# Attention and a squared-ReLU FFN on one core: the ffn matmuls read their moving columns in pairs, one from each half of the block

## The chip, the cores and the metric

The kernel runs on one core of a Trainium2 chip. The time is that of one execution on the device in microseconds; the median of several runs is given. TensorE (PE) multiplies: a matmul loads a stationary operand of up to 128 x 128 (the weights; PEld in the profile) and streams the columns of a moving operand past it, and the sums go into a PSUM bank of 512 float32 columns. VectorE (DVE) and ScalarE (ACT) do the elementwise work, read PSUM and write SBUF. SyncE (SP) issues most of the transfers to and from HBM. Each engine works through its own list of instructions in order, and they wait for each other through semaphores.

## The reference

Cut to what is computed:

```python
# q, k, v: (8, 12, 448, 64)
scores = scale * np.matmul(q, k.transpose(0, 1, 3, 2)) - np.log(448)
attn = 1.0 / (1.0 + np.exp(-scores))
attn_out = np.matmul(attn, v)
x = attn_out.transpose(0, 2, 1, 3).reshape(3584, 768)
# w_in: (768, 2048), w_out: (2048, 768), s, b: one number each
h = x @ w_in
r = np.maximum(h, 0.0)
g = s * (r * r) + b
out = g @ w_out          # (3584, 768)
```

## The kernel before

**Attention** (lines 344 to 632) runs over 24 quads of heads (8 batches x 3). For each quad it makes the scores (line 420), the sigmoid on ScalarE (line 400), the product with the values (lines 454 and 463), and stores the result as x in HBM (line 471), one row of the feature dimension per partition, tokens along the free dimension. Beside it VectorE and ScalarE convert the weights and make sums of weight blocks, which go to HBM.

**The ffn** works on blocks of 512 tokens (`TB`), seven in all. Every operand is float32 that is split into a high part, rounded to a type that TensorE reads at full rate (`F32R`), and a low part, the rest. A product of two such numbers is three matmuls: high by high, high by low, low by high (`PARTS`).

Block 0 goes the plain way. `ffn1` (line 556) makes one row block of h from 6 blocks of 128 features x 3 parts, 18 matmuls, for each of 16 row blocks of the hidden layer (line 563). `activate` (line 751) makes g of it. `ffn2` (line 761) adds g into six PSUM banks `pos`, 18 matmuls again (line 765). At the end ScalarE copies the six banks out, in pairs (lines 844 to 847), and the pool of banks is opened anew for the next stage.

Blocks 1 to 6 go in two groups of three (`threes`). For each group the matrix product is made by a scheme with 15 products of sums of blocks in place of 18. The first layer (lines 1080 to 1127) has 15 products in four pieces `p`, 60 units of 12 matmuls (line 1095: 2 halves `j` x 2 feature blocks `c` x 3 parts), in the order `L1`. A unit reads one tile of weight sums, `wu`, which `weights()` (line 864) takes from a ring of seven tiles that are fetched six units ahead (`AHEAD`). Products that share a bank pair follow each other in it (`CHAINS_1`), and `results_1` (line 960) copies or adds the bank into the tiles `G`. The second layer (lines 1210 to 1251) has 60 units of 12 matmuls too (line 1225), in the order `L2`: 15 products, each with its four pieces one after the other. `prep` (line 1016) makes the operand sums and splits them three units ahead (`LEAD`). When a product is done, `results_2` (line 1138) copies or subtracts its bank pair (`bk`, 128 x 2 x 512) into the output tiles `C`, and `out_store` (line 836) sends them to HBM. There are four bank pairs.

The last unit of all (`end`) is cut into three pieces (`LAST`, line 875): feature block 0 with 512 columns, and feature block 1 in two halves of 256. Each piece has a bank pair of its own, is subtracted from `C["t"]` and stored by itself (lines 1231 to 1237), so that the end of the kernel is short.

The moving operand of each ffn matmul is 512 neighbouring float32 words of each partition: `x0[h][xi][:, cc, :]` (line 564), `g[:, gi, :]` (line 766), `opd[i][xi][:, c, :]` (line 1096), `g[gi][:, f, tk]` (line 1226). The column of the PSUM bank is that of the token.

The helpers `add` and `sub` (lines 177 to 181) are where VectorE's additions and subtractions are recorded, so those rows have lines 178 and 181; ScalarE's copies of banks in `results_2` have line 1141, its split casts lines 678 and 680.

Of the kernel before, what the change touches and what calls it, by code (L numbers as in the profile page):

```python
# [36 lines left out]
TB = 512  # L37
# [57 lines left out]
def sigmoid_attention_relu2_ffn(  # L95
# [10 lines left out]
    nc = tc.nc  # L106
# [7 lines left out]
    KC = NCC // 3  # L114
# [59 lines left out]
    def f32(ap):  # L174
        return ap.bitcast(F32)

    def add(o, x, y):
# [378 lines left out]
    def ffn1(f, w):  # L556
        ph = ps_h.tile([P, TB], F32, tag="ph", name=f"ph_{f}")
        m = 0
        for c in range(NCC):
            h, cc = divmod(c, HC)  # L560
            k, kc = divmod(c, KC)
            for wi, xi in PARTS:
                nc.tensor.matmul(  # L563
                    ph, w[:, k, wi, kc * P : (kc + 1) * P], x0[h][xi][:, cc, :],
                    start=m == 0, stop=m == 3 * NCC - 1,
                )
                m += 1
        cx.free(w)
        return ph
# [191 lines left out]
    def ffn2(w, g, first, last):  # L761
        for e in range(NCC) if not last else evict:
            k, kc = divmod(e, KC)
            for i, (wi, gi) in enumerate(PARTS):
                nc.tensor.matmul(  # L765
                    pos[e], w[:, k, wi, kc * P : (kc + 1) * P], g[:, gi, :],
                    start=first and i == 0, stop=last and i == 2,
                )
# [75 lines left out]
    for e in evict[::2]:  # L844
        outs.append(slot(f"o_{e}"))
        nc.scalar.copy(outs[-1][:, 0], pos[e])
        nc.scalar.copy(outs[-1][:, 1], pos[e + 1])
    todo[10].pop(0)()
# [102 lines left out]
    for n, blocks in enumerate(threes):  # L951
# [128 lines left out]
        for u, (i, p) in enumerate(L1):  # L1080
# [10 lines left out]
            for j in range(2):  # L1091
                m = 0
                for c in range(KC):
                    for wi, xi in PARTS:
                        nc.tensor.matmul(  # L1095
                            bk[:, j], wt[:, j, wi, c * P : (c + 1) * P], opd[i][xi][:, c, :],
                            start=i == ch[0] and m == 0,
# [39 lines left out]

        def results_2(i, bk):
            def copy(c):
                C[c] = slot(f"C_{n}_{c}")  # L1140
                nc.scalar.copy(C[c], bk)

# [12 lines left out]
            elif i == 10:  # L1155
                sub(C[5], C[5], bk)
                put(5)
            elif i == 7:
                C[2] = slot(f"C_{n}_2")
                sub(C[2], C["u"], bk)  # L1160
                copy(0)
                put(2)
            elif i == 1:
                sub(C[0], bk, C[0])
                put(0)
# [4 lines left out]
            elif i == 4:  # L1170
                sub(C[8], bk, C[8])
            elif i == 3:
                sub(C[7], C[7], bk)
                put(7, True)
            elif i == 12:
                C[1] = C.pop("u")
                sub(C[1], bk, C[1])
                put(1)
            elif i == 11:
                C[3] = slot(f"C_{n}_3")  # L1180
                sub(C[3], C["t"], bk)
                put(3)
            elif i == 14:
                copy("v")
            elif i == 0:
                sub(C["v"], C["v"], bk)

# [11 lines left out]
            elif n + 1 < len(threes):  # L1199
                C[4] = C.pop("t")  # L1200
                for e in range(KC):
                    sub(C[4][:, e], C[4][:, e], bk[:, e])
                    m, k = divmod(4, 3)
# [6 lines left out]
        for j, (i, p) in enumerate(L2):  # L1210
# [8 lines left out]
            for e, tk in LAST if end else [(e, slice(TB)) for e in range(KC)]:  # L1219
# [3 lines left out]
                for f in range(2):  # L1223
                    for m, (wi, gi) in enumerate(PARTS):
                        nc.tensor.matmul(  # L1225
                            o, wt[:, f, wi, e * P : (e + 1) * P], g[gi][:, f, tk],
                            start=(end or i == ch[0] and p == 0) and f == 0 and m == 0,
# [3 lines left out]
                if end:  # L1231
                    x = C["t"][:, e, tk]
                    sub(x, x, o)
                    t0 = blocks[1] * TB
                    nc.sync.dma_start(
                        out[(KC + e) * P : (KC + e + 1) * P, t0 + tk.start : t0 + tk.stop], x
                    )
            if n + 1 == len(threes) and j + 2 == len(L2):
                sub(C["t"], C["t"], bk)
            for t in g:  # L1240
# [49 lines left out]
```

## Time and profile before

| what | value |
|---|---|
| median of 3 runs | 1039.26 us (1038.59 to 1039.77) |
| span of the profiled execution | 1037.5 us |
| attention, from the first score to the last product with the values | 3.91 to 250.73 us |
| block 0 of the ffn | 250.73 to 381.56 us |
| blocks 1 to 3, first and second layer | 381.56 to 544.76 and to 707.96 us |
| blocks 4 to 6, first and second layer | 707.96 to 871.16 and to 1034.44 us |
| HBM read and written | 198.18 and 88.08 MB |

The stages are read from the chain of waits in order of time. In the profile a row of a group names the line, the engine, the operation, what it writes and reads, the shapes and the count, then the busy time of the group in us and the mean of one in ns, then the idle time of the engine just before and what ended it. In a row of a stretch each engine has its busy time and, in brackets, its instructions; behind them stand the granted TensorE clock (1.00 is full), the share of the DMA engines and their GB/s. Matmuls are pipelined: their durations overlap, so the pace of TensorE is read from one start to the next. The page's line PEclk is the granted clock in 40 slices of the span, in tenths.

### The profile page before, as it was taken

The numbers are of one execution on the slowest core, as the hardware profiler recorded it, in microseconds if no ns is written. First come the engines' busy times: TensorE is split into PE (matmuls) and PEld (weight loads), VectorE is DVE, ScalarE is ACT, GpSimd is POOL, SyncE is SP. The second block draws the span as 40 slices with busy tenths as digits, with TensorE's granted clock in tenths as the row PEclk, the third lists the DMA queues.
The fourth block names the chain that finished last, engine by engine and source line by source line (L and its number), as shares of the span: only waits on it lengthen the run. The fifth ranks groups of instructions, "written<-read, shape, count | busy, mean of one in ns | idle before, by whom it ended". The sixth has DMA issues, their size and how long they took to land.

```text
span 1037.5 us, 13898 instructions
## 1 busy us (share of the span) xinstructions
PE 1033.7 (100%) x5288; PEld 780.3 (75%) x5288; DVE 836.1 (81%) x906; ACT 617.2 (59%) x666; POOL 0.2 (0%) x4
## 2 busy tenths in 40 slices
PE   9999999999999999999999999999999999999998
PEld 4545555555888888888888888888888888888887
DVE  5999999995988965898898897796455789888777
ACT  7999999988776755564445344344445335552432
POOL 0000000000000000000000000000000000000000
PEclk9999999999999999999999999999999999999999
DMA  9788989995999999999686676897666666676773
GB/s 327 269 331 342 360 317 393 346 396 194 332 366 367 358 408 410 341 341 322 201 269 189 218 229 220 291 317 249 197 190 195 194 193 197 190 236 207 222 228 118
DMA packets 101568, 287.16 MB, mean 277 GB/s; under 512 B 10240, under 2 KB 20352, under 8 KB 101504
## 3 DMA queue, kind: packets, MB, share of 16 engines
q1 hardware_dynamic: 101216, 285.84, 79.6%
q8 instruction: 42, 0.69, 0.3%
q10 hardware_dynamic: 288, 0.46, 0.1%
q14 instruction: 22, 0.18, 0.0%
HBM read 198.18 MB, written 88.08 MB: 276 GB/s over the span
## 4 chain that ended last, share of the span: by engine, by line
PE 100%; DVE 0%; issue 0%
PE o L1225 31%; PE h L1095 31%; PE pav L454 11%; PE psc L420 9%; PE ph L563 6%; PE po L765 6%; PE psc_l L441 2%; PE pav L463 2%; PE psc L426 0%; PE idle L482 0%; DVE C_t L181 0%
## 5 line engine op out<-in xcount | busy, mean ns | idle before, releaser
L1095 PE MATMUL h<-s_1h,wu 128*128 128x512 f32 x480 | 148.0, 389 | 0.0
L1095 PE MATMUL h<-s_0h,wu 128*128 128x512 f32 x480 | 147.8, 389 | 0.0
L400 ACT ACTIVATE a<-psc,nls 128x896 f32<-128x896 f32 x144 | 132.7, 1008 | 12.9 <-PE psc L420 10.1
L454 PE MATMUL pav<-a,v 128*64 128x448 f32 x576 | 113.8, 543 | 0.0
L1095 PEld LDWEIGHTS h<-s_1h,wu 128*128 128x128 f32 x480 | 90.1, 188 | 18.8
L1095 PEld LDWEIGHTS h<-s_0h,wu 128*128 128x128 f32 x480 | 90.1, 188 | 18.6
L968 ACT COPY G<-h 128x1024 f32<-128x1024 f32 x48 | 48.8, 1017 | 85.5 <-PE h L1095 57.8
L860 ACT ACTIVATE G<-G,b_sb,s_sb 128x1024 f32<-128x1024 f32 x48 | 59.8, 1246 | 61.4 <-DVE G L857 60.7
L1095 PE MATMUL h<-s_0l,wu 128*128 128x512 f32 x240 | 93.4, 389 | 0.0
L1095 PE MATMUL h<-s_1l,wu 128*128 128x512 f32 x240 | 93.4, 389 | 0.0
L454 PEld LDWEIGHTS pav<-a,v 128*64 128x64 f32 x576 | 39.1, 137 | 63.8 <-issue 45.4
L178 DVE TENSOR_TENSOR G<-G,h 128x1024 f32<-128x1024 f32 x40 | 48.8, 1219 | 39.4 <-PE h L1095 39.3
L1225 PE MATMUL o<-g_3h,wu 128*128 128x512 f32 (+1 forms) x244 | 79.0, 385 | 0.0
L1225 PE MATMUL o<-g_0h,wu 128*128 128x512 f32 x240 | 78.8, 389 | 0.0
L1225 PE MATMUL o<-g_1h,wu 128*128 128x512 f32 x240 | 78.8, 389 | 0.0
L1225 PE MATMUL o<-g_2h,wu 128*128 128x512 f32 x240 | 78.8, 389 | 0.0
L765 PE MATMUL po<-g,w 128*128 128x512 f32 x288 | 67.7, 389 | 0.0
L765 PEld LDWEIGHTS po<-g,w 128*128 128x128 f32 x288 | 54.1, 188 | 11.2
L563 PE MATMUL ph<-x0h,w 128*128 128x512 f32 x192 | 61.7, 390 | 0.0
L420 PE MATMUL psc<-qkh 64*128 64x448 f32 x282 | 54.1, 380 | 0.0
L1225 PEld LDWEIGHTS o<-g_3h,wu 128*128 128x128 f32 x244 | 45.6, 188 | 9.2
L1095 PEld LDWEIGHTS h<-s_0l,wu 128*128 128x128 f32 x240 | 45.0, 188 | 9.4
(152 smaller groups left out, 2028.0 us busy)
## 6 DMA issues: line engine op xcount, KB each, us to landing
wu<-wd SPq DMA_DIRECT2D x240, 512.0 KB, 3.6
wd<-t SPq DMA_DIRECT2D x36, 768.0 KB, 8.6
qk<-qk_t SPq DMA_DIRECT2D x23, 896.0 KB, 7.4
st<-w_out SPq DMA_DIRECT2D x16, 768.0 KB, 10.3
st<-w_in SPq DMA_DIRECT2D x16, 768.0 KB, 9.3
wd<-w SPq DMA_DIRECT2D x16, 768.0 KB, 5.6
v<-v_t SPq DMA_DIRECT2D x24, 448.0 KB, 6.1
xd<-xo SPq DMA_DIRECT2D x24, 448.0 KB, 4.9
```

What stands on the lines that cost most here:

```text
L178: nc.vector.tensor_tensor(o, x, y, op=ALU.add)
L400: nc.scalar.activation(a, psc[:, :, :S], AF.Sigmoid, bias=nls, scale=SCALE)
L420: nc.tensor.matmul(o[:, j, :S], two[wi][r, i, cols], two[xi][r, i, :S], start=m == 0, stop=m == 2,)
L441: nc.tensor.matmul(psc[half[i], j, :S], x[r, i, 1, 3 * P :], x[r, i, 0, :], start=True, stop=True,)
L454: nc.tensor.matmul(pav[r, i, :S], ld_[1][:, 3 * i + c, j, :], a[i, c][:, j, :], start=c == 0, stop=False,)
L463: nc.tensor.matmul(pav[r, i, :S], ld_[1][half[i], 6, j, :], a[half[i], j, :], start=False, stop=True,)
L563: nc.tensor.matmul(ph, w[:, k, wi, kc * P : (kc + 1) * P], x0[h][xi][:, cc, :], start=m == 0, stop=m == 3 * NCC - 1,)
L765: nc.tensor.matmul(pos[e], w[:, k, wi, kc * P : (kc + 1) * P], g[:, gi, :], start=first and i == 0, stop=last and i == 2,)
L860: nc.scalar.activation(x, x, AF.Identity, bias=b_sb, scale=s_sb)
L968: nc.scalar.copy(g(m, h), bk)
L1095: nc.tensor.matmul(bk[:, j], wt[:, j, wi, c * P : (c + 1) * P], opd[i][xi][:, c, :], start=i == ch[0] and m == 0, stop=m == 3 * KC - 1, sk ...
L1225: nc.tensor.matmul(o, wt[:, f, wi, e * P : (e + 1) * P], g[gi][:, f, tk], start=(end or i == ch[0] and p == 0) and f == 0 and m == 0, stop ...
```

## The change

The moving operand of every ffn matmul is given another order of columns: column 0, column 256, column 1, column 257 and so on, by a view of the tile with two dimensions. (In the last two pieces, of 256 columns, the halves are of 128.) The tiles in SBUF stay as they are. PSUM column 2b + a then holds token 256a + b. The first layer's results are written to `G` in that order and nothing is turned back there. The second layer reads `G`'s tiles in pairs again, so its banks hold the tokens turned by two bits: PSUM column 4b + a holds token 128a + b. Where the second layer's banks are read (the copies out of block 0, `results_2`, the last subtractions), the views are made so that the output tiles have the tokens in order. The number of instructions of each kind stays the same. In the last unit each of the two pieces of feature block 1 now holds 128 tokens of the block's first half and 128 of its second, so each is stored as two runs of 128 tokens.

```diff
+    def paired(ap):
+        return ap.rearrange("p (a b) -> p b a", a=2)
+
+    def runs(ap, n):
+        return ap.rearrange("p j (a b) -> p j a b", a=n)
+
+    def turned(ap, n):
+        return ap.rearrange("p j (b a) -> p j a b", a=n)
...
-                    ph, w[:, k, wi, kc * P : (kc + 1) * P], x0[h][xi][:, cc, :],
+                    ph, w[:, k, wi, kc * P : (kc + 1) * P], paired(x0[h][xi][:, cc, :]),
...
-                    pos[e], w[:, k, wi, kc * P : (kc + 1) * P], g[:, gi, :],
+                    pos[e], w[:, k, wi, kc * P : (kc + 1) * P], paired(g[:, gi, :]),
...
-        nc.scalar.copy(outs[-1][:, 0], pos[e])
-        nc.scalar.copy(outs[-1][:, 1], pos[e + 1])
+        for k in range(2):
+            nc.scalar.copy(runs(outs[-1], 4)[:, k], pos[e + k].rearrange("p (b a) -> p a b", a=4))
...
-                            bk[:, j], wt[:, j, wi, c * P : (c + 1) * P], opd[i][xi][:, c, :],
+                            bk[:, j], wt[:, j, wi, c * P : (c + 1) * P],
+                            paired(opd[i][xi][:, c, :]),
...
         def results_2(i, bk):
+            bk = turned(bk, 4)
+
+            def c4(c):
+                return runs(C[c], 4)
+
             def copy(c):
                 C[c] = slot(f"C_{n}_{c}")
-                nc.scalar.copy(C[c], bk)
+                nc.scalar.copy(c4(c), bk)
...
             elif i == 10:
-                sub(C[5], C[5], bk)
+                sub(c4(5), c4(5), bk)
                 put(5)
...
-                            o, wt[:, f, wi, e * P : (e + 1) * P], g[gi][:, f, tk],
+                            o, wt[:, f, wi, e * P : (e + 1) * P], paired(g[gi][:, f, tk]),
...
                 if end:
-                    x = C["t"][:, e, tk]
-                    sub(x, x, o)
-                    t0 = blocks[1] * TB
-                    nc.sync.dma_start(
-                        out[(KC + e) * P : (KC + e + 1) * P, t0 + tk.start : t0 + tk.stop], x
-                    )
+                    x = C["t"][:, e]
+                    dst = out[(KC + e) * P : (KC + e + 1) * P, blocks[1] * TB : (blocks[1] + 1) * TB]
+                    if tk.stop - tk.start == TB:
+                        x4 = x.rearrange("p (a b) -> p a b", a=4)
+                        sub(x4, x4, o.rearrange("p (b a) -> p a b", a=4))
+                    else:
+                        h = tk.start * 2 // TB
+                        x, dst = (y.rearrange("p (d h b) -> p h d b", d=2, h=2)[:, h] for y in (x, dst))
+                        x4 = x.rearrange("p d (a b) -> p d a b", a=2)
+                        sub(x4, x4, o.rearrange("p (b d a) -> p d a b", d=2, a=2))
+                    nc.sync.dma_start(dst, x)
             if n + 1 == len(threes) and j + 2 == len(L2):
-                sub(C["t"], C["t"], bk)
+                ct = runs(C["t"], 4)
+                sub(ct, ct, turned(bk, 4))
```

The other branches of `results_2` are changed in the same way as `i == 10`.

More of the change, by code (lines that the diff above doesn't have):

```diff
@@ L1159, in results_2 @@
                 C[2] = slot(f"C_{n}_2")
-                sub(C[2], C["u"], bk)
+                sub(c4(2), c4("u"), bk)
                 copy(0)
@@ L1163, in results_2 @@
             elif i == 1:
-                sub(C[0], bk, C[0])
+                sub(c4(0), bk, c4(0))
                 put(0)
@@ L1170, in results_2 @@
             elif i == 4:
-                sub(C[8], bk, C[8])
+                sub(c4(8), bk, c4(8))
             elif i == 3:
-                sub(C[7], C[7], bk)
+                sub(c4(7), c4(7), bk)
                 put(7, True)
@@ L1176, in results_2 @@
                 C[1] = C.pop("u")
-                sub(C[1], bk, C[1])
+                sub(c4(1), bk, c4(1))
                 put(1)
@@ L1180, in results_2 @@
                 C[3] = slot(f"C_{n}_3")
-                sub(C[3], C["t"], bk)
+                sub(c4(3), c4("t"), bk)
                 put(3)
@@ L1185, in results_2 @@
             elif i == 0:
-                sub(C["v"], C["v"], bk)
+                sub(c4("v"), c4("v"), bk)
                 def eight():
@@ L1201, in results_2 @@
                 for e in range(KC):
-                    sub(C[4][:, e], C[4][:, e], bk[:, e])
+                    sub(c4(4)[:, e], c4(4)[:, e], bk[:, e])
                     m, k = divmod(4, 3)
```

## The prediction

> **What bounds the kernel now.** I read the page's busy shares and slices first, then the chain of waits in order of time, then stretches of the span, and last single start times of matmuls.
>
> ```profile
> span 1037.5 us, 13898 instructions
> PE 1033.7 (100%) x5288; PEld 780.3 (75%) x5288; DVE 836.1 (81%) x906; ACT 617.2 (59%) x666; POOL 0.2 (0%) x4
> PEclk9999999999999999999999999999999999999999
> PE 100%; DVE 0%; issue 0%
> PE o L1225 31%; PE h L1095 31%; PE pav L454 11%; PE psc L420 9%; PE ph L563 6%; PE po L765 6%; PE psc_l L441 2%; PE pav L463 2%; PE psc L426 0%; PE idle L482 0%; DVE C_t L181 0%
> ```
>
> TensorE is busy in the whole span, and the chain that ended last is TensorE alone. The four ffn lines (563, 765, 1095, 1225) have 74% of it. No other engine sets an end, so the change is worth what it does to the time of one ffn matmul, unless another engine or the DMA becomes late. The chain in order of time gives the ffn part exactly:
>
> ```profile
> 250.73 8.43 PE ph L563 x36
> 259.16 4.08 PE po L765 x18
> ...
> 373.40 8.16 PE po L765 x36
> 381.56 163.20 PE h L1095 x720
> 544.76 163.20 PE o L1225 x720
> 707.96 163.20 PE h L1095 x720
> 871.16 163.28 PE o L1225 x726
> 1034.44 0.02 issue
> 1034.46 0.42 DVE C_t L181
> ```
>
> From 250.73 to 1034.44 us the chain holds only ffn matmuls, without a gap. 163.20 us by 720 is 226.67 ns from one start to the next. How many there are: 16 x 18 in the first layer of block 0, 16 x 18 in its second, and 3 x 720 + 726 behind, 3462 in all. 3450 of them have 512 columns, the last 12 have 256.
>
> What the 226.67 ns consist of is seen by comparing streams. These are single rows of the timeline (start, duration, what); two matmuls on two halves of the array, started within some ns, make one row of x2:
>
> ```profile
> 1032.95 0.28 PE L1225 MATMUL o<-g_3l,wu 128*128 128x256 f32 x1
> 1034.15 0.28 PE L1225 MATMUL o<-g_3h,wu 128*128 128x256 f32 x1
> 139.55 0.36 PE L420 MATMUL psc<-qkl,qkh 64*128 64x448 f32 x2
> 142.79 0.36 PE L420 MATMUL psc<-qkh,qkl 64*128 64x448 f32 x2
> 143.53 0.55 PE L454 MATMUL pav<-a,v 128*64 128x448 f32 x2
> 147.29 0.55 PE L454 MATMUL pav<-a,v 128*64 128x448 f32 x2
> ```
>
> - 256 columns: ten starts from 1032.95 to 1034.15, 120.0 ns each. Against 226.67 ns for 512, 256 more columns cost 106.67 ns, which is 0.4167 ns a column. 512 columns take 213.33 ns, and **13.33 ns remain in every ffn matmul, long or short**.
> - Scores (line 420, the same rounded type): 16 steps of a pair from 139.55 to 142.79, 202.5 ns each; 448 columns take 186.67, and 15.8 remain.
> - Attention times values (line 454, plain float32): ten steps from 143.53 to 147.29, 376.0 ns. Here a column takes two slots, 448 x 0.8333 = 373.33 ns, and **only 2.67 remain**.
>
> So the remainder is large where the moving operand is read at one column per 0.4167 ns and small where it is read at half that rate. Weight loads run beside all of these:
>
> ```profile
> L1095 PEld LDWEIGHTS h<-s_1h,wu 128*128 128x128 f32 x480 | 90.1, 188 | 18.8
> L454 PEld LDWEIGHTS pav<-a,v 128*64 128x64 f32 x576 | 39.1, 137 | 63.8 <-issue 45.4 <-ACT a L400 18.2 <-ACT a_l L400 0.2
> ```
>
> 64 columns of weights more take 51 ns more, so a 128-column load reads for about 100 ns of the 226.67, while the moving columns stream. I read the 13.33 ns as the moving stream stopped by the reading of weights, which at half rate fits between. The other reading is a fixed cost of switching 128-column weights (line 454 has 64). No row decides between them.
>
> **The change part by part.**
>
> *The moving reads* (lines 563, 765, 1095, 1225). No matmul is added or removed; the same 512 columns stream in another order, 0, 256, 1, 257 and so on. No row shows a moving operand read in anything but unit steps, so I bound one matmul. From below: 213.33 ns, the remainder gone. From above: each column takes two slots, as in line 454, 426.67 + 2.67 = 429.3 ns. Between them lie 216.0 (213.33 and the remainder of line 454) and 226.67 (nothing changes). I take 216.0. The reason is a guess at the mechanism: one column per 0.4167 ns is twice the rate at which line 454 reads, so I suppose that two half-rate reads serve alternate columns. In unit order both walk over the whole block in steps of two; in paired order each walks through one half without a gap and needs half as many accesses, which leaves room for the weights. The gain is 226.67 - 216.0 = 10.67 ns by 3462, **36.9 us**. With the whole remainder gone it is 46.2 us, with half of it 23.1, and at the upper bound the cost is 202.7 ns by 3462, 702 us.
>
> [...]
>
> *The bank reads of the second layer.* Banks come out in an order turned by two bits, so ScalarE and VectorE read them in steps of four words (16 bytes), in runs of 128. Per group of three blocks that is 7 copies by ScalarE and 9 or more subtractions by VectorE, and 6 copies for block 0. The writes stay in long runs.
>
> ```profile
> L208 DVE SCALAR_TENSOR_TENSOR wf<-st,wf 128x768 int32<-128x768 int32 x32 | 30.4, 950 | 0.0
> L181 DVE TENSOR_TENSOR w<-wf,w 128x768 fp32r<-128x768 f32 x32 | 29.9, 954 | 3.8 <-ACT w L314 3.5
> L1141 ACT COPY C<-o 128x1024 f32<-128x1024 f32 x8 | 8.1, 1017 | 42.3 <-PE o L1225 38.7 <-DVE C L181 3.6
> L181 DVE TENSOR_TENSOR C<-C,o 128x1024 f32<-128x1024 f32 x4 | 4.9, 1220 | 11.0 <-PE o L1225 11.0
> 871.16:1034.44 163.28, 163.26 (x726) 135.23 (x725) 134.66 (x119) 66.93 (x66) 0.00 (x0) 1.00 0.64 200
> ```
>
> Line 208 reads every second word and takes 950 ns where line 181 takes 954 in unit steps: a step of 8 bytes is free. A step of 16 bytes is not shown. Bounds: nothing, and twice the time (1.22 us more for a subtraction). I take nothing, by the nearest row. Its cover: a bank is written again at the earliest one product (4 x 12 matmuls, 10.9 us) after its read. If all is doubled, VectorE has 134.66 + 11 x 1.22 = 148 us in the last stage, which the faster TensorE would end in 726 x 0.216 = 157: it fits, narrowly.
>
> ```profile
> 381.80 0.57 ACT L846 COPY o<-po 128x512 f32<-128x512 f32 x1
> 382.27 0.59 ACT L847 COPY o<-po 128x512 f32<-128x512 f32 x1
> 1031.67 2.49 DVE L181 TENSOR_TENSOR C_t<-C_t,o 128x1024 f32<-128x1024 f32 x3 [1.26 <-PE o L1225]
> ```
>
> Two places have less cover. The second bank pair of the new first layer opens 12 matmuls after 381.56, at 384.28 (384.15 when faster), and the first two copies out of block 0 end at 382.86; doubled, about 383.9. Still in time. The second is the end: the last four subtractions follow each other from 1031.67. Doubled they would end near 1036.9 in place of 1034.88, **2.0 us at most**, taken as nothing. The last two stores go out in runs of 128 columns in place of 256; their bytes are the same.
>
> *What is late next.* A stage that is 4.7% shorter has the same bytes to move:
>
> ```profile
> 308.12:332.60 24.48, 24.48 (x109) 20.27 (x109) 20.11 (x36) 16.46 (x24) 0.00 (x0) 1.00 1.00 370
> 381.56:463.16 81.60, 81.60 (x361) 67.57 (x361) 61.01 (x68) 49.97 (x59) 0.00 (x0) 1.00 0.97 368
> 463.16:544.76 81.60, 81.60 (x361) 67.57 (x361) 72.75 (x74) 39.02 (x39) 0.00 (x0) 1.00 0.80 269
> DMA to landing us min/median/max: 3.3/3.6/9.5
> ```
>
> The DMA engines are full (share 1.00 and 0.97) from about 283 to 463 us and free again after. Were they the bound there, 4.7% of 180 us, 8.4 us, of the gain would be lost. The fetches of weights land within 9.5 us at worst and are issued six units of 12 matmuls ahead (`AHEAD`), 6 x 12 x 0.2267 = 16.3 us, so I take nothing, and keep 8.4 for the range.
>
> **The sum.** 1037.5 - 36.9 = 1000.6 us of span; the median of the runs, 1039.26, lies 1.8 above the profiled span, so 1039.26 - 36.9 = **1002.3 us**.
>
> **The rivals.**
>
> 1. *The read order costs nothing and brings nothing.* The 13.33 ns is the switch of weights, the same for 512 and 256 columns, which a read order can't touch. For it: it does not grow with the moving columns, and line 420, which also loads 128 weight columns, has it too. Against it: line 454, with half the weight columns, would keep half of it, 6.7 ns, and keeps 2.67. Time: 1039, within 0.2% (1037.2 to 1041.3; a measurement of this kernel can tell about that much from no change).
> 2. *The paired read halves the moving rate.* TensorE would fetch two neighbouring columns in one access, and a pair that lies 1 KB apart takes two. It decides as soon as two such accesses take over 0.83 ns. Price: 429.3 ns a matmul, 1039.3 + 702 = 1741 us, or some part of it. For it: one column per 0.4167 ns was never seen here but in unit steps. Against it: nothing in this trace reads moving columns otherwise.
> 3. *TensorE keeps its pace and the turned bank reads are late.* Twice the bank reads give 2.0 us at the end and up to 5 more if VectorE falls behind in the two second-layer stages (it has 28.6 us to spare in the last): 1041.3 to 1048. For it: VectorE is at 81% of the span. Against it: it never released TensorE.
>
> **How the numbers follow.** Forecast, remainder mostly gone: 0.57, its own range 993 (46.2 us gained) to 1021 (half of the 36.9 us; a full DMA, which takes 8.4, lies inside). Rival 1: 0.18. Rival 2: 0.18. Rival 3: 0.07. The range runs from 993 to 1048 and leaves out rival 2, 0.18. Faster by over 0.2% is the forecast, 0.57; within 0.2% is rival 1, 0.18; slower is rivals 2 and 3, 0.25.
>
> **What would show it.** Right: the stages of 720 matmuls take 155.5 us in place of 163.20, the step from start to start is near 216 ns, line 420 keeps its 202.5 and line 454 its 376. Rival 1: the 163.20 stays. Rival 2: a step well over 226.67, up to 429 ns, with every other engine idle. Rival 3: TensorE shows idle time behind VectorE, or the last subtraction ends over 1 us after the last matmul. If copies at line 1141 stay at 1.02 us and the subtractions at 1.22, the 16-byte step is free. The forecast is wrong if the remainder does not depend on how the moving operand is read.

## The result, and the profile after

The changed kernel takes **1008.33 us** (1007.67 to 1009.56, four runs) against 1038.92 (1038.31 to 1039.77, four runs) for the kernel before: a ratio of 0.9707, with an interval of 0.9693 to 0.972. That is 30.6 us faster. The profiled executions show 31.6 (spans of 1037.5 and 1005.9; the changed kernel's is that of its fastest run), and the rest of this section divides those.

Lines have moved: the ffn matmuls are now lines 572, 774, 1104 and 1240, scores 429, values 463, ScalarE's bank copies 1156 (second layer), 856 (block 0) and 977 (first layer), VectorE's additions 187 and subtractions 190, the fetch of weights 672.

The page of the changed kernel: span, busy shares, and the shares of the engines in the chain that ended last.

```profile
span 1005.9 us, 13900 instructions
PE 998.8 (99%) x5288; PEld 785.2 (78%) x5288; DVE 836.4 (83%) x906; ACT 616.9 (61%) x666; POOL 0.2 (0%) x4
PE 86%; DMA 6%; DVE 5%; ACT 1%; issue 1%; SPq 1%; DVEq 0%; ACTq 0%
```

Before, the chain was TensorE alone. Now 14% of it belongs to transfers and their issue, VectorE and ScalarE, although TensorE is busy 99% of the span. Both are true: wherever TensorE waits even once for another engine, the chain is followed back through that engine, and may stay there for a long stretch in which TensorE ran too. A share of the chain is no lost time. The same chain in order of time (start, duration, what) shows where it leaves TensorE:

```profile
383.26 8.43 DMA wu<-wd
391.75 0.81 issue
392.56 1.01 ACT G L977
393.61 142.05 PE h L1104 x648
535.66 124.53 PE o L1240 x576
...
691.70 155.40 PE h L1104 x720
847.10 155.66 PE o L1240 x726
```

The first layer of blocks 4 to 6 has 155.40 us for its 720 matmuls (before 163.20), **215.83 ns** from start to start. The first starts of the stages, from the timeline (start, duration, what):

```profile
375.09 0.38 PE L1104 MATMUL h<-s_0h,wu 128*128 128x512 f32 x1
535.50 0.38 PE L1240 MATMUL o<-g_0h,wu 128*128 128x512 f32 x1
691.54 0.38 PE L1104 MATMUL h<-s_1h,wu 128*128 128x512 f32 x1
846.94 0.38 PE L1240 MATMUL o<-g_0h,wu 128*128 128x512 f32 x1
```

Block 0 starts at 249.98 us (before 250.66), and the last matmul of all at 1002.47 (before 1034.15). From start to start:

| stage | before, us | after, us | at the new pace |
|---|---|---|---|
| block 0, 576 matmuls | 130.73 | 125.10 | 124.32 |
| blocks 1 to 3, first layer | 163.20 | **160.41** | 155.40 |
| blocks 1 to 3, second layer | 163.20 | 156.04 | 155.40 |
| blocks 4 to 6, first layer | 163.20 | 155.40 | 155.40 |
| blocks 4 to 6, second layer, to the start of the last matmul | 163.15 | 155.53 | 155.33 |

At the new pace the 3450 long matmuls gain 10.83 ns each, and the 12 short ones 8 ns (112.0 from start to start, before 120.0): 37.5 us. 6.6 of these are lost again, 5.0 of them in one stage. (The ffn also begins 0.7 us earlier, which is not the change's doing: its start lay between 249.5 and 250.9 us in the profiles of kernels with the same attention.) The next rows are stretches of that stage (length, then busy time and instructions of PE, PEld, DVE, ACT, POOL, the granted clock, the DMA share and GB/s), and single rows of its timeline:

```profile
380.00:400.00 20.00, 17.18 (x72) 14.38 (x72) 8.40 (x7) 9.96 (x11) 0.00 (x0) 0.91 1.05 408
390.63:393.61 2.98, 0.16 (x1) 0.00 (x0) 0.93 (x1) 2.01 (x3) 0.00 (x0) 1.00 1.04 398
394.15:397.36 3.21, 3.21 (x9) 2.51 (x8) 0.36 (x1) 0.32 (x1) 0.00 (x0) 0.53 1.05 398
```

```profile
390.41 0.38 PE L1104 MATMUL h<-s_0h,wu 128*128 128x512 f32 x1
393.61 0.48 PE L1104 MATMUL h<-s_0h,wu 128*128 128x512 f32 x1 [2.82 <-ACT G L977]
391.60 1.04 ACT L687 CAST s_0h<-a 128x1024 fp32r<-128x1024 f32 x1 [4.94 <-DMA a<-xd]
392.56 1.92 ACT L977 COPY G<-h 128x1024 f32<-128x1024 f32 x2
```

```profile
382.13 1.03 SPq L346 DMA_DIRECT2D a<-xd  x2
```

TensorE stands still for 3.0 us at 390.63, before the seventh unit (unit 6, counted from 0), and then runs 3.2 us at a granted clock of 0.53. The gap (2.98) and the slow clock (eight steps of 427 ns in place of 216, 1.7 us) make 4.7 of the 5.0; the first step behind the gap (0.1 us longer) and a short stop at 410.73 us (0.2) are the rest. Read the rows from there backwards: unit 6 waits for a bank copy by ScalarE (line 977); ahead of that copy on ScalarE stands a cast, and the cast waited 4.94 us for a load, `a<-xd`, which SP issued at 382.13 (the last row, SP's queue). (The chain above names a fetch of weights, `wu<-wd`, that landed at 391.69; the cast was running by then, so it is the load that held it.) The same cast and the same issue in the kernel before:

```profile
393.42 1.05 ACT L678 CAST s_0h<-a 128x1024 fp32r<-128x1024 f32 x1
```

```profile
384.02 1.04 SPq L337 DMA_DIRECT2D a<-xd  x2
```

There unit 6 was due at 381.39 + 72 x 0.22667 = 397.71. Less the cast (1.05) and one copy (1.02), that left 397.71 - 393.42 - 2.07 = 2.2 us of slack. After the change TensorE comes to unit 6 at 390.63, 7.1 us earlier, but the load is issued only 1.9 and the cast starts only 1.8 us earlier. 7.08 - 1.82 - 2.22 = 3.0, the gap. The load was not slower (9.0 us from issue to landing, before and after): it didn't move up with TensorE, and the slack that had hidden this is used up. The other 1.6 us are five short stops, at 265.6, 351.3, 540.7, 685.9 and 852.1 us, of 0.1 to 0.4 us with 0.1 more in the next step, and the first step of the ffn, which is 0.1 longer, as it was before. At two of the five, 351.3 and 685.9, the profile names VectorE as waited for.

Last, the bank reads, as groups (busy us, mean ns, idle time before and what ended it):

```profile
L1156 ACT COPY C<-o 128x1024 f32<-128x1024 f32 x8 | 8.1, 1016 | 37.1 <-PE o L1240 34.6 <-DVE C L190 2.6
L190 DVE TENSOR_TENSOR C<-C,o 128x1024 f32<-128x1024 f32 x4 | 4.9, 1221 | 7.9 <-PE o L1240 7.9
```

1016 and 1221 ns where reading in unit steps took 1017 and 1220: reading a bank in steps of 16 bytes cost nothing here.

### The profile page after: what moved, and what is told of

It reads as the page before. It is cut to its first block, busy times and chain, and to the rows that moved or that the text cites. A ratio compares the mean times of both kernels' runs of the same rounds, so it can differ in the third digit from the quotient of the medians.

```text
span 1005.9 us, 13900 instructions
## 1 busy us (share of the span) xinstructions
PE 998.8 (99%) x5288; PEld 785.2 (78%) x5288; DVE 836.4 (83%) x906; ACT 616.9 (61%) x666; POOL 0.2 (0%) x4
## 4 chain that ended last, share of the span: by engine, by line
PE 86%; DMA 6%; DVE 5%; ACT 1%; issue 1%; SPq 1%; DVEq 0%; ACTq 0%
PE h L1104 30%; PE o L1240 28%; PE pav L463 11%; PE psc L429 9%; DMA wd<-t 3%; PE psc_l L450 2%; PE ph L572 2%; PE pav L472 2%; PE po L774 1%; DVE t L190 1%; DVE w L190 1%; DMA wu<-wd 1%; DMA wd<-td 1%; DMA wd<-w 1%; DMA a<-xd 0%
## 5 line engine op out<-in xcount | busy, mean ns | idle before, releaser
L1104 PE MATMUL h<-s_0h,wu 128*128 128x512 f32 x480 | 144.6, 382 | 2.8 <-ACT G L977 2.8
L1104 PE MATMUL h<-s_1h,wu 128*128 128x512 f32 x480 | 142.9, 379 | 0.0
L1104 PE MATMUL h<-s_1l,wu 128*128 128x512 f32 x240 | 91.0, 379 | 0.0
L1240 PE MATMUL o<-g_3h,wu 128*128 128x512 f32 (+1 forms) x244 | 76.4, 376 | 0.0
L1240 PE MATMUL o<-g_1h,wu 128*128 128x512 f32 x240 | 76.3, 379 | 0.0
L1240 PE MATMUL o<-g_0h,wu 128*128 128x512 f32 x240 | 76.3, 379 | 0.0
L1240 PE MATMUL o<-g_2h,wu 128*128 128x512 f32 x240 | 76.3, 379 | 0.0
L187 DVE TENSOR_TENSOR G<-G,h 128x1024 f32<-128x1024 f32 x40 | 48.7, 1217 | 31.6 <-PE h L1104 30.5
L774 PE MATMUL po<-g,w 128*128 128x512 f32 x288 | 65.1, 380 | 0.2 <-DVE g L190 0.2
L429 PE MATMUL psc<-qkl,qkh 64*128 64x448 f32 x282 | 51.5, 362 | 0.0
L429 PE MATMUL psc<-qkh,qkl 64*128 64x448 f32 x282 | 51.4, 361 | 0.0
```

Source lines behind the costliest of these rows:

```text
L187: nc.vector.tensor_tensor(o, x, y, op=ALU.add)
L429: nc.tensor.matmul(o[:, j, :S], two[wi][r, i, cols], two[xi][r, i, :S], start=m == 0, stop=m == 2,)
L774: nc.tensor.matmul(pos[e], w[:, k, wi, kc * P : (kc + 1) * P], paired(g[:, gi, :]), start=first and i == 0, stop=last and i == 2,)
L1104: nc.tensor.matmul(bk[:, j], wt[:, j, wi, c * P : (c + 1) * P], paired(opd[i][xi][:, c, :]), start=i == ch[0] and m == 0, stop=m == 3 * KC ...
L1240: nc.tensor.matmul(o, wt[:, f, wi, e * P : (e + 1) * P], paired(g[gi][:, f, tk]), start=(end or i == ch[0] and p == 0) and f == 0 and m == ...
```

## Experiments on the reading order

The theory of the prediction (A), a guess: two readers at half rate serve alternate columns, and weights are read where their accesses leave room. Rivals: any view with two dimensions is fast (B); successive columns must lie far apart (C); or the remainder is a fixed switch of weights that the new order happens to hide. These three kernels have other orders in the last four stages; a helper `moving(n, l, t, c)` picks them by group `n` and layer `l`. All banks are read as in the changed kernel, so what they hold is another order of tokens, or other sums where the operand itself is another.

```diff
+        if (n, l) == (0, 0):
+            return t[:, :, : TB // 2]
+        if (n, l) == (0, 1):
+            return t[:, c, :].rearrange("p (b a) -> p a b", a=2)
+        if (n, l) == (1, 0):
+            return t[:, c, :1].to_broadcast([P, TB])
+        if (n, l) == (1, 1):
+            return t[:, c, :]
```

> As the changed kernel, but in the four stages of 720 matmuls the moving columns are read in other orders, so those results are permuted or wrong: first layer of blocks 1 to 3: two unit runs of 256, one from each of two feature blocks (a view of two dimensions that is not paired); second layer of blocks 1 to 3: all even columns, then all odd ones; first layer of blocks 4 to 6: one and the same column 512 times; second layer of blocks 4 to 6: unit order as in the kernel before. Step from start to start in each, in this order. Theory A (two half-rate reads serve alternate columns, and what counts is how many separate accesses each makes, since the weights need room between them): 226.7 ns; over 226.7, up to 430 ns, since each read then moves on by four words per access; 215.8; 226.7. Theory B (any view of two dimensions is read in a faster way, whatever its order): 215.8; 215.8; 215.8 or 226.7; 226.7. Theory C (two columns that follow each other must lie far apart): 226.7; 226.7 or more; 226.7 or more; 226.7. If the 13.3 ns were a switch of weights that the paired order hides in some other way, the one column read 512 times keeps 226.7.

Its single starts and its chain:

```profile
500.07 0.39 PE L1120 MATMUL h<-s_0l,wu 128*128 128x512 f32 x1
502.79 0.39 PE L1120 MATMUL h<-s_0l,wu 128*128 128x512 f32 x1
```

```profile
542.17 326.39 PE o L1256 x720
868.56 155.40 PE h L1120 x720
1023.96 163.18 PE o L1256 x726
```

Two unit runs of 256, a view with two dimensions, keep the old step: 12 steps in 2.72 us, 226.7 ns. So B falls. 512 times the same column gives 215.8, so the fixed switch falls: with the same weights loads, the remainder goes from 13.33 to 2.5 ns when the moving stream is one column. All even columns and then all odd ones give 453.3 ns, twice the step of unit order.

```diff
+        if (n, l) == (0, 0):
+            return t[:, c, :].rearrange("p (a b) -> p b a", a=4)
+        if (n, l) == (0, 1):
+            return t[:, c, :].rearrange("p (a b c) -> p b a c", a=2, c=2)
+        if (n, l) == (1, 0):
+            return t[:, c, :].rearrange("p (b a c) -> p b c a", a=2, c=4)
+        if (n, l) == (1, 1):
+            return t[:, c, :].rearrange("p (b a c) -> p b c a", a=2, c=2)
```

> As the changed kernel, but in the four stages of 720 matmuls the moving columns are read in other orders, so those results are permuted: first layer of blocks 1 to 3: one column from each quarter in turn (0, 128, 256, 384, 1, ...); second layer of blocks 1 to 3: two neighbours from one half, two from the other (0, 1, 256, 257, 2, ...); first layer of blocks 4 to 6: pairs within groups of eight (0, 4, 1, 5, 2, 6, 3, 7, 8, ...); second layer of blocks 4 to 6: pairs within groups of four (0, 2, 1, 3, 4, ...). Theory A (two reads for alternate columns, each gaining by neighbours; assumed: an access brings four words): each read hops at every access in the first and second stage, so 226.7 ns or more, up to 430; in the third each read walks through four neighbours and then four others, 215.8; in the fourth it makes as many accesses as in unit order, 226.7, or 215.8 if an access brings only two words. Theory B (any order in two or more dimensions is fast): 215.8 in all four. Theory C (columns that follow each other must lie far apart): 215.8; about 221; 215.8; 226.7.

Its chain:

```profile
375.11 203.99 PE h L1120 x720
579.10 244.81 PE o L1256 x720
823.90 155.40 PE h L1120 x720
979.30 163.19 PE o L1256 x726
```

Columns 0, 128, 256, 384, 1 and so on: 283.3 ns. 0, 1, 256, 257: 340.0. Groups of eight, 0, 4, 1, 5, 2, 6, 3, 7: 215.8. Groups of four, 0, 2, 1, 3: 226.7. C falls with the first and the second, for which it expected 215.8 and about 221. Pairs four words apart are as fast as pairs 256 words apart (215.8 ns both). The last two orders differ in how many neighbouring words every second column walks through: four at 215.8 ns, two at 226.7.

```diff
+        if (n, l) == (0, 0):
+            return t[:, c, :]
+        if (n, l) == (1, 0):
+            return t[:, :, : TB // 2].rearrange("p a b -> p b a")
+        if (n, l) == (1, 1):
+            return t[:, c, :].rearrange("p (a b) -> p b a", a=8)
+        return paired(t[:, c, tk])
+
+    def stepped(n, ap, c):
+        if n == 0:
+            return ap.rearrange("p (b a) -> p a b", a=2)[:, c]
+        return ap[:, c * P : (c + 1) * P]
```

> As the changed kernel, but: blocks 1 to 3 load every second column of the weights in place of 128 neighbours (the results of these blocks are wrong), the first layer with the moving columns in unit order, the second with paired ones; first layer of blocks 4 to 6: pairs with one column from each of two feature blocks, 512 words apart; second layer of blocks 4 to 6: one column from each of eight eighths in turn (both permuted). Theory A (reading the weights stops the moving stream, and the 13.3 ns are its accesses): stepped weights make twice the accesses, so about 240 ns in unit order (13.3 twice) and 215.8 to 229 in paired order; pairs from two feature blocks 215.8; eighths 226.7 or more, up to 430, since each read hops. Theory of a fixed switch, with a moving order that hides it: 226.7, 215.8, 215.8, 215.8. Theory C (columns that follow each other must lie far apart): 226.7, 215.8, 215.8, 215.8.

In its first layer of blocks 1 to 3 both operands are told apart: a matmul loads every second column of the 256 of its weights (steps of 8 bytes) and reads the moving columns in unit order; in the second layer the weights are stepped in the same way and the moving columns go in pairs. Single starts, then its chain:

```profile
500.02 0.40 PE L1120 MATMUL h<-s_0l,wu 128*128 128x512 f32 x1
504.22 0.39 PE L1120 MATMUL h<-s_0l,wu 128*128 128x512 f32 x1
...
999.65 0.69 PE L1256 MATMUL o<-g_0h,wu 128*128 128x512 f32 x1
1002.57 0.69 PE L1256 MATMUL o<-g_1h,wu 128*128 128x512 f32 x1
```

```profile
545.45 137.28 PE o L1256 x636
...
701.29 155.40 PE h L1120 x720
```

18 steps in 4.20 us are 233.3 ns: with stepped weights the remainder beside a unit order grows from 13.33 to 20.0 ns. With paired columns the same weights leave the step at 215.8. So what stepped weights cost depends on the order of the columns; that the two readings get in each other's way, and that the paired order leaves room, is the author's estimate from these steps. The size was missed: twice the remainder would have been 240. Pairs from two feature blocks give 215.8 too, eighths 487 (6 steps in 2.92 us).

All orders beside each other, with the accesses for 512 columns that A counts if an access brings four neighbouring words and the even and the odd columns of the stream have a reader each:

| order of the columns | accesses by A | ns a matmul |
|---|---|---|
| one column 512 times | 2, always the same words | 215.8 |
| pairs from two halves, from two feature blocks, or groups of eight | 128 | 215.8 |
| unit order, two unit runs, groups of four | 256 | 226.7 |
| quarters | 512 | 283.3 |
| 0, 1, 256, 257 | 512 | 340.0 |
| evens, then odds | 512 | 453.3 |
| eighths | 512 | 487 |

The count sorts fast, old and slow orders without a miss. It doesn't say how slow the slow ones are: four orders with the same count lie between 283 and 487 ns, and nothing here tells what sets that. The readers and the four words are the author's estimate: when every second column walks through two neighbours a matmul takes 226.7 ns, through four 215.8, and through 256 (pairs from two halves) no less. No row shows an access or a reader.

## The scores in pairs

The scores (line 429) read the same rounded type in unit order, so A has them gain too. Here they read pairs 224 apart, the plain float32 ones (line 450, and line 435 at the start) too, since all go into the same sums over tokens, and the result is turned back where x is copied out.

```diff
-                            o[:, j, :S], two[wi][r, i, cols], two[xi][r, i, :S],
+                            o[:, j, :S], two[wi][r, i, cols], paired(two[xi][r, i, :S]),
...
-                    psc[half[i], j, :S], x[r, i, 1, 3 * P :], x[r, i, 0, :],
+                    psc[half[i], j, :S], x[r, i, 1, 3 * P :], paired(x[r, i, 0, :]),
...
-        nc.vector.tensor_copy(o, pav[:, :, :S])
+        nc.vector.tensor_copy(runs(o, 2), turned(pav[:, :, :S], 2))
```

> The changed kernel, with the scores' moving columns paired as well (224 apart, rounded type and plain float32 alike), and the copy of attention's result out of PSUM turned back. Theory A (what a matmul loses in unit order is the weights' reading): a pair of scores takes 191.7 ns in place of 202.5 in the rounded type; 423 such pairs give 4.6 us, so the ffn begins near 245.5 us in place of 250.05; the plain float32 streams, which have only 2.7 ns over their columns, keep theirs. What the whole gains depends on the next stretch: with theory D (the DMA engines are the bound from about 283 to 460 us and before) most of the 4.6 us is lost there again, 1005 to 1009 us, ratio 0.968 to 0.971; if they are not, 1003.7 us, ratio 0.966. Rival for the attention: ScalarE, busy 94% of that stage, holds it, and the ffn begins within 1 us of 250.

1011.35 us, ratio 0.9736 (0.9721 to 0.975): slower than the changed kernel. Single starts of its scores, and its group of float32 scores; then the same group before:

```profile
131.31 0.35 PE L429 MATMUL psc<-qkh,qkl 64*128 64x448 f32 x2
133.58 0.35 PE L429 MATMUL psc<-qkh,qkl 64*128 64x448 f32 x2
...
L450 PE MATMUL psc_l<-qk 64*64 64x448 f32 x192 | 28.1, 656 | 0.0
```

```profile
L441 PE MATMUL psc_l<-qk 64*64 64x448 f32 x192 | 23.6, 562 | 0.0
```

Twelve steps in 2.27 us are 189.2 ns for a pair of scores, 448 columns (186.67) and 2.5: as A expected, a third kind of matmul gains, which had 202.5. But a plain float32 matmul gets slower in paired order, 656 ns in place of 562; eight of them, from the first start to that of the next group, take 0.99 us in place of 0.80. A's readers were drawn from the float32 products having the smaller remainder; that they lose by the same order was foreseen by no theory and stays open. The chain of waits in attention, TensorE alone before, now goes through ScalarE's sigmoids in almost every quad, which the faster scores don't shorten (six of them 5.50 us, in the changed kernel 5.54), and the slower float32 products lie on it too. The ffn began at 253.6 us in place of 250.0.

## Where 5 us of the gain went

Kernels shown above say where the slack before unit 6 went. In `e1_forms`, `e3_weights` and `e2_hops` block 0 is as in the changed kernel, so TensorE reaches the first layer of blocks 1 to 3 at about 375 us (before 381.39), but its steps there are 226.7, 233.3 and 283.3 ns. Waits of TensorE in `e1_forms` from 375 to 546 us:

```profile
PE h L1120 <- ACT G L993: 2.3, 1, 2.3
PE h L1120 <- DVE G L203: 0.9, 1, 0.9
```

At the old step of 226.7 ns the gap before unit 6 is there too, 2.5 us (391.34 to 393.84), and the stage takes 167.0 us, more than before. In `e3_weights` it is 1.9 us, and in `e2_hops`, where unit 6 is due at 395.4 us, there is none. So the gap comes from TensorE reaching this stage 6.4 us earlier, most of it the gain of block 0, and not from the shorter steps of the stage itself.

Two readings of the gap at unit 6: a single one, made by the order on ScalarE (S), or the first of what transfers that come too late can stop anywhere in this stage (D for the bytes, Q for SP's order). Each kernel below is the changed one with the edit shown.

```diff
-        0: (13,), 1: (13, 2), 2: (13, 2), 3: (2, 1), 4: (1,), 5: (8,), 6: (8,), 7: (8,), 8: (8,),
+        0: (13,), 1: (13, 2), 2: (13, 2), 3: (2,), 5: (1, 8), 6: (1, 8), 7: (8,), 8: (8,),
...
-                if u < 4 and fn.__name__ == "hi":
+                if u < 8 and fn.__name__ == "hi":
```

> As the changed kernel, but the cast and the split of product 1's operand in the first layer of blocks 1 to 3 are asked for two units later, and casts of the first eight units are put behind the bank copies on ScalarE. Theory S (the 3.0 us gap at 390.4 us is ScalarE held by a load that lands at 391.6, with the bank copy that TensorE needs queued behind it, and the half clock from 394 to 397.5 follows from the gap): no gap over 0.5 us, granted clock 1.000, 1003.4 us (1008.3 less 3.0 and 1.95), ratio to the kernel before 0.966. Rival (the DMA engines are the bound of this stretch, so the wait comes back one or two products later, with the same half clock): 1007 to 1009 us, ratio 0.969 to 0.971.

The cast of the late load now stands behind the bank copies. Waits of its TensorE (line, for what: us in total, times, longest), from 360 to 480 us:

```profile
PE h L1104 <- DVE G L187: 3.2, 1, 3.2
PE h L1104 <- ACT G L977: 1.3, 1, 1.3
```

The gap at unit 6 is gone, and two others are there, at units 10 and 12. The stage takes 161.98 us. S falls: the edit moved the wait, it didn't remove it. Four more kernels move stores and sums. `e7_spread` has the edit above and holds block 0's stores until unit 16 and two groups of weight sums 6 and 4 units longer; `e8_both` adds the paired scores to it; `e10_hold` holds the stores until unit 44, and `e11_hold_later` does so beside the edit above.

```diff
-    4: (6, 9, 9, 10, 11, 11, 11, 12, 13, 13, 14, 14),
-    5: (14, 17, 17, 18, 19, 19, 19, 20, 21, 23, 24, 24),
+    4: (12, 15, 15, 16, 17, 17, 17, 18, 19, 19, 20, 20),
+    5: (18, 21, 21, 22, 23, 23, 23, 24, 25, 27, 28, 28),
...
-            if outs and u > 4:
+            if outs and u > 16:
```

> The kernel of the run before last (product 1's cast later), with transfers moved out of the full stretch: the three stores of block 0 wait until unit 16 in place of 4, and the sums of weights of the second layer that read back from HBM begin 6 and 4 units later (pieces 4 and 5). Theory D (the gap is bytes: 3 x 512 KB of stores and 4 x 384 KB of loads, about 3.1 MB, at 405 GB/s 7.6 us of the DMA engines, stand before loads that TensorE needs): no gap over 1 us, granted clock 1.000, first layer of blocks 1 to 3 in 155.4 to 157 us in place of 160.4, about 1003.5 us, ratio 0.966. Rival (a single late load, whatever stands before it): a gap of 2 to 4 us again at the products behind, with the half clock, 1007 to 1010 us, ratio 0.969 to 0.972.

> Both of the two together: scores paired, and the transfers spread. Theories A and D: 1003.5 less up to 4.6 us, 999 to 1003 us, ratio 0.962 to 0.966. If the bytes of the attention and of block 0 are the bound, nothing is gained over the run with the transfers spread, 1003 to 1005 us.

> The changed kernel with the three stores of block 0's results (1.5 MB) held back to units 45 to 47, behind the full stretch; nothing left out. Theory D: they are 3.9 us of the DMA engines, but they were issued from 395 us on, behind the gap at 390 us, so that gap (3.0 us and the half clock, 1.95 us) stays and only what comes behind it goes, some tenths of a us: 1007 to 1008.5 us, ratio 0.969 to 0.971. If they did stand in the way of the loads: 1004 us.

> The same with product 1's cast two units later (as in the first of the two runs on the gap), which by itself moved the gap from unit 6 to units 10 and 12, both behind 395 us. Theory D: with 1.5 MB less in front of units 10 and 12, 3.9 us of the DMA engines, most of the 5.3 us of gaps and the half clock go: first layer of blocks 1 to 3 in 156 to 158 us in place of 162, 1004 to 1006 us, ratio 0.966 to 0.969. Rival (the full stretch goes on to 480 us whatever is held back): gaps at later units as with the spread transfers, 1008 to 1010 us.

None of the four is faster than the changed kernel (table below). The stage of `e10_hold`, the slowest, loses 11.9 us: 6.8 in gaps before units 6, 18 and 28, and 5.1 at half clock behind the first two of them. Why the later gaps come wasn't settled. To take bytes away instead of moving them, one kernel leaves out four stores of weight sums, 2.1 MB in all; product 10 of the first layer then reads another row in their place.

```diff
-        nc.sync.dma_start(wd[l][p][:, 9], f32(t).rearrange("p j h c -> p j (h c)"))
+        if l:
+            nc.sync.dma_start(wd[l][p][:, 9], f32(t).rearrange("p j h c -> p j (h c)"))
...
-            row = ROWS[l].index((FIRST, SECOND)[l][i][0])
+            row = ROWS[l].index((FIRST, SECOND)[l][i][0]) if l or i != 10 else 0
```

> The changed kernel without the four stores of one sum of first-layer weights (row d, 4 x 512 KB = 2.1 MB, issued while block 0 runs); product 10 reads row 0 in its place, so the first layer's results are wrong. Nothing else is moved. Theory D (the loss of some 6 us between 283 and 480 us is bytes): 2.1 MB at 405 GB/s are 5.2 us of the DMA engines, so the first layer of blocks 1 to 3 takes 156 to 157 us in place of 160.4, no gap over 1 us at the sixth unit, clock 1.000, about 1003.5 us, ratio 0.965 to 0.967. Rival (the order in which ScalarE and VectorE wait for single loads, not the bytes): the gap at the sixth unit stays over 2 us, 1007 to 1009 us.

Its waits of TensorE from 360 to 560 us, and two of its stretches:

```profile
PE h L1105 <- ACT G L978: 1.7, 1, 1.7
PE h L1105 <- DVE G L187: 1.7, 1, 1.7
```

```profile
360.00:380.00 20.00, 20.00 (x95) 17.50 (x94) 13.32 (x16) 12.58 (x20) 0.00 (x0) 1.00 1.05 404
380.00:400.00 20.00, 18.26 (x85) 15.69 (x84) 8.96 (x8) 11.25 (x12) 0.00 (x0) 1.00 1.04 397
```

The stage takes 159.34 us, the shortest of all, and still 3.9 too long; the ratio of the whole, 0.9697, can't be told from the changed kernel's 0.9707. TensorE's waits, 3.4 us, are no shorter than the changed kernel's 2.8: what the stage has over it is the clock, which stayed at 1.00, where the changed kernel lost 1.7 us at half clock. The DMA engines stay full here (1.05 and 1.04): with those stores gone, other transfers fill them, and the loads that the stage waits for still lie among them. D, which expected 156 to 157 us, isn't borne out.

The last two kernels put the loads ahead of the fetch of weights in SP's queue, one by one or all four at once.

```diff
             wt = weights()
-            if n == 0 and u < 4:
-                load_raw(0, *start[5 + u])
```

(In `e12_loads_first` these two lines stand above `wt = weights()`; in `e13_all_first` all four loads stand there at `u == 0`.)

> The changed kernel, with each of the four token loads of the first units issued ahead of that unit's fetch of weights, not behind it. Theory Q (the gap at 390.4 us comes from the order in SyncE's queue: at unit 0 the fetch of weights holds the queue 5.4 us, until the store that it reads, issued at 372.9, has landed at 380.7, and the load that product 1's cast waits for is issued behind it): that load is issued near 375.3 us and lands near 384, no gap at unit 6, clock 1.000; the other three loads still come behind that fetch, so some gap may stay at units 10 to 12, under 2 us. 1003.5 to 1006 us, ratio 0.966 to 0.968. Theory D (bytes alone): the gap stays or moves, 1007 to 1010 us.

> The same with all four token loads (2 MB) issued at unit 0 ahead of its fetch. Theory Q: none of the four waits behind the store, so the gaps at units 6 and 12 both go, unless the fetch of the weights for unit 6, now behind 2 MB of loads, is itself late (needed at 390.6 us; 2 MB at 405 GB/s are 5.2 us, so it should land near 389): about 1003.5 us, ratio 0.966. Theory D (bytes alone): 1007 to 1010 us.

The loads stand in SP's queue behind a fetch of weights, and this one behind a store, for 5.4 us in the kernel before and in the changed one alike. Waits of SP's queue in the changed kernel, 366 to 396 us:

```profile
SPq L672 <- DMA wd<-t: 5.4, 1, 5.4
```

The held fetch goes out when the store has landed, in the changed kernel and in the one before at:

```profile
380.72 0.33 SPq L672 DMA_DIRECT2D wu<-wd  x1
```

```profile
382.55 0.33 SPq L663 DMA_DIRECT2D wu<-wd  x1
```

These are 1.8 us apart, and so the load behind it moved up by only 1.9. But the fetch that is held is issued ahead of unit 0, so both kernels brought the first load forward by only 0.15 us (to 381.98 and 382.00, from 382.13): a load ahead of the held fetch, which Q asks for, was not tested. `e13_all_first` did bring the other loads forward (all were issued by 389.7 us), and then weights came too late, which is the wait of its TensorE from 360 to 560 us:

```profile
PE h L1105 <- DMA wu<-wd: 5.1, 1, 5.1
```

| kernel | ratio to before, interval | first layer, blocks 1 to 3, us | TensorE's waits in it, us |
|---|---|---|---|
| changed kernel | 0.9707 (0.9693 to 0.972) | 160.41 | 2.8 |
| `e4_later` | 0.972 (0.9704 to 0.9737) | 161.98 | 4.5 |
| `e5_scores` | 0.9736 (0.9721 to 0.975) | 160.52 | 4.5 |
| `e7_spread` | 0.9725 (0.9709 to 0.9742) | 161.36 | 4.1 |
| `e8_both` | 0.9747 (0.9733 to 0.9762) | 162.26 | 4.5 |
| `e9_fewer` (leaves stores out) | 0.9697 (0.9683 to 0.9712) | 159.34 | 3.4 |
| `e10_hold` | 0.9759 (0.9741 to 0.9777) | 167.30 | 6.3 |
| `e11_hold_later` | 0.9723 (0.9707 to 0.9739) | 161.97 | 5.4 |
| `e12_loads_first` | 0.9719 (0.9706 to 0.9732) | 161.78 | 4.5 |
| `e13_all_first` | 0.9734 (0.9721 to 0.9747) | 162.92 | 5.1 |

Beside the waits the stage loses time at half clock, which the edits don't aim at: one stretch of 3.4 us in the changed kernel, `e4_later`, `e8_both` and `e12_loads_first`, one of 6.8 in `e13_all_first`, 10.2 in two in `e10_hold`, none in the others.

These arrangements move the wait to other units and other waiters (ScalarE's copies, VectorE's sums, the weights), and no complete kernel among them has a shorter stage than the changed one. Those whose DMA was read over 380 to 480 us (`e5_scores` and `e8_both` were not) have shares of 0.95 to 1.00 there, in `e10_hold` 0.90, as the kernel before has 0.97. The gap at unit 6 of the changed kernel is traced to one load and the store in front of it; that the stage would lose as much in any case, because the DMA as a whole is full (share 1.01 from 360 to 480 us in the changed kernel), isn't shown: `e9_fewer` doesn't favour it, no run had the DMA clearly below full there and all loads in time, and none issued that load ahead of the held fetch.

## Why the prediction was right, and where it missed

- **"I take 216.0. The reason is a guess at the mechanism."** Measured 215.83: the remainder went from 13.33 to 2.5 ns, 37.5 us in all where 36.9 were forecast. (The 12 matmuls of 256 columns keep 5.3 ns, 112.0 less 106.67; why they keep more wasn't tested.) The supposed mechanism, fewer accesses that leave room for the weights, passed tests that could have felled it: the repeated column (215.8 ns), groups of eight against groups of four (215.8 and 226.7), stepped weights (233.3 in unit order, 215.8 in pairs). Not foreseen was how much slower the orders are for which it counts more accesses (453.3 and 487 ns, where the expectations stopped at 430), and that float32 loses (656 ns a matmul in place of 562). That there are two readers for alternate columns is inferred from these times and stays a model.
- **Rival 1, a fixed switch of weights**, is out: the same loads, 215.8 ns with a repeated column. Its argument that the remainder doesn't grow with the moving columns was true (13.33 ns with 512 and with 256) and decided nothing: the weights, on which A puts it, are the same for 256 columns.
- **Rival 2, paired halves the rate**, is out: the very pair that was to take two accesses is fast (215.83 ns). What it feared, an order that doubles the time, is real for other orders: evens before odds cost 453.3 ns, more than the upper bound of 429.3.
- **The bank reads, "I take nothing, by the nearest row"**: right, 1016 and 1221 ns. The last subtraction starts 0.31 us behind the start of the last matmul (1002.78 and 1002.47) and takes 0.42, as before (1034.46 and 1034.15). So rival 3 is out. (Its upper end of 1048 isn't its own sum either: 2.0 and 5 on 1039.3 are 1046.3.) Scores kept their 202.5 ns in the changed kernel.
- **"What is late next … so I take nothing, and keep 8.4 for the range"** is the step that failed in size. Of the 37.5 us, 5.0 were given back in the first layer of blocks 1 to 3 and 1.6 in the other stages. The stretch was the right one. The argument that put the term at nothing looked only at the fetches of weights with their six units of lead. What came late was a load of an operand, with a cast on ScalarE behind it and bank copies behind the cast. Nor was the reason for the worry, a stage that is 4.7% shorter with the same bytes, what the first gap needed: `e1_forms` has it at the old step, because block 0 ends sooner. That the load had 2.2 us of slack, that ScalarE takes cast and copy in this order, and that SP issues the load behind a fetch which waits 5.4 us for a store could be read in the trace of before.

37.5 less 6.6, and 0.7 for the earlier start, is 31.6 us, which the profiles show; the medians show 30.6.

## What to carry to other kernels

When a matmul's step is longer than its columns, compare several streams of the same kernel (long and short, other types) and ask what is left over per matmul; then try orders of the moving columns, since the order alone made 4.8% of a matmul here, or doubled it (453.3 ns for 226.67). Measure the order for the type at hand: what helped the rounded type (215.83 ns for 226.67) hurt plain float32 (656 for 562). And when the bound engine becomes faster, walk through each thing that it waits for with the new times, loads with the casts and copies queued behind them included, not only the stream that has a lead built in.

## What the hardware showed besides

- After the gap of 3.0 us, of which the profile counts 2.8 as a wait, the granted clock fell to half for 3.4 us (0.50 from 394.37 to 397.78): matmuls that start at 394.80, 395.23, 396.08 and on to 397.36 are 427 ns apart (6 steps in 2.56 us). In `e10_hold` even a wait of 1.9 us was followed by a slow stretch (the 84 matmuls from 430.52 took 20.10 us, where 84 steps of 215.83 ns are 18.13; granted clock 0.91 from 420 to 440), while one of 2.9 us in `e5_scores` and two of 1.7 us in `e9_fewer` left the mean clock of the run at 1.000. So in these runs the length of a wait alone doesn't decide.
- So 1.7 us were lost at half clock behind 3.0 us of standing still, and the stage lost 1.7 times the gap.

```profile
394.80 0.63 PE L1104 MATMUL h<-s_0l,wu 128*128 128x512 f32 x1
395.23 1.06 PE L1104 MATMUL h<-s_0h,wu 128*128 128x512 f32 x2
397.36 0.58 PE L1104 MATMUL h<-s_0l,wu 128*128 128x512 f32 x1
```
